# Values, states and the places of the down projections in a gated linear attention kernel with a SoLU block

## The chip, the cores and the metric

The kernel runs on one core of a Trainium2 chip. A time is device microseconds of one execution, from its start to its end. The profile is of one other execution of the same program on the same kind of chip, taken by the hardware profiler. PE is the engine for matrix products, DVE, ACT and POOL work on vectors, SP issues transfers.

## The reference

A recurrent attention with a gate for every key channel, then a two-layer block whose hidden values pass through a SoLU (value times softmax) and a layer norm. B=4 batches, H=8 heads, S=768 tokens, D=48 channels; 3072 tokens of 384 values, 1024 hidden.

```python
for t in range(S):
    state = alpha[:, :, t, :, None] * state + np.einsum('bhd,bhe->bhde', k[:, :, t], v[:, :, t])
    y[:, :, t] = np.einsum('bhd,bhde->bhe', q[:, :, t], state)
x = y.transpose(0, 2, 1, 3).reshape(B * S, H * D)
h = x @ w_in
e = np.exp(h - np.max(h, axis=-1, keepdims=True))
solu = h * (e / (np.sum(e, axis=-1, keepdims=True) + 1e-09))
mu = np.mean(solu, axis=-1, keepdims=True)
var = np.mean((solu - mu) ** 2, axis=-1, keepdims=True)
out = (solu - mu) / np.sqrt(var + 1e-06) * g_ln @ w_out
```

## The kernel before

The sequence is cut into G=6 chunks of 128 tokens; a chunk holds four batches, so 512 tokens. Within a chunk the attention is done by products: scaled queries times scaled keys, masked (`scores`, `masked`, giving sT), times v (`read_values`), plus scaled queries times the state of the chunks before (`read_state`). Both add into four PSUM banks y, one for each batch; ACT copies them to x. `next_state` multiplies the keys (turned back by `keys_back`) with v into two PSUM banks kv and adds them to the state; `decay` on POOL multiplies the state with the chunk's gate.

A head's 48 key channels don't fit 32 rows. They are kept as 32 firsts and 16 lasts; two heads' lasts share 32 rows, so there are H=8 blocks of firsts and NP=4 of lasts, NB=12 in all. On the side of the values, vn and the state have 80 columns for a head: 32 firsts, 16 zeros, 16 lasts, 16 zeros. `last` takes 32 columns that hold a head's lasts at the one end or the other, zeros at the rest, so that two heads add into the same 32 rows of y. The state has 16 blocks: 8 for the firsts of the keys, 8 for the lasts, where a pair of heads has both heads' keys in its rows; `apart` makes queries qv with zeros in the other head's rows from qe, which holds both. `read_state(n)`, n = 0 to 3, does one group of y's rows: n = 0, 1 the firsts of the values, n = 2, 3 the lasts of even and odd heads. A matrix product in fp32 stands in the profile as two matmuls and two weight loads.

The block after it: `up(g, f)`, f = 0 to 7, makes 128 hidden channels of chunk g for its 512 tokens (3 products of 512 columns), ACT takes the exponential, DVE multiplies it with h to u, ACT squares u. `running` sums over f on POOL and DVE, `token_sums` adds up over channels on PE. `down(n, half)` makes one batch's 128 tokens n of the output from four of the eight u blocks (4 products of 385 columns); `finish(n)` scales and stores it, for chunk 0 to 4 by SP.

Order is written out by hand; each engine runs its instructions in the order in which the program issues them. A prologue does chunk 0's attention, its ups and downs, and chunk 1's attention up to `next_state(1)`. Then the loop over g = 1 to 5, here called periods, does eight steps each: up(g, s), with work of the attention of chunk g+1 placed by a plan (`first` for period 1, `second` for 2, `usual` for 3 and 4; period 5 has none), and one half down of chunk g-1 per step, from the list `todo`. Within a step the places are head, up, finish, token sums, behind, running sums, middle, down, tail. Periods 2 to 5 thus hold eight half downs, period 1 none, and chunk 5's eight come after the loop, with the last chunk's token sums and norm behind the first.

In the old plans the values and the new state stand at step 7's tail, after the down; the new state is made for the last chunk too. The keys, with loading of v (`load_v`, by SP), come at step 0 behind the up.

Names and lines: down 471 to 480 (matmul 477), up_mm 366, up_act 380 to 382, running 394 and 397, scores 268, masked 279, keys_back 287 and 289, the matmuls of read_state and read_values both 300 (in `y_mm`), x copies 331, next_state 342 and 351, decay 251 and 254, queries 244, key transposes on DVE 184 and 187, scans 209, load_v 170.

Of the kernel before, what the change touches and what calls it, by code (L numbers as in the profile page):

```python
# [32 lines left out]
def fast_path(ctx, tc, q, k, v, alpha, moe_w_in, moe_w_out, moe_g_ln, out):  # L33
# [133 lines left out]
    def load_v(g):  # L167
        t = slice(g * P, (g + 1) * P)
        for dst, src in ((slice(0, E0), slice(0, E0)), (slice(48, 64), slice(E0, D))):
            nc.sync.dma_start(  # L170
                out=vn[:, :, :, dst].rearrange("p b h d -> p (b h) d"),
                in_=v[:, :, t, src].rearrange("b h p d -> p (b h) d"),
            )

    def load_v_first(slot):
        x = slots[slot].rearrange("p (n d) -> p n d", d=D)
        y = vn.rearrange("p b h d -> p (b h) d")
        nc.sync.dma_start(out=x, in_=v[:, :, 0:P].rearrange("b h p d -> p (b h) d"))
        for dst, src in ((slice(0, E0), slice(0, E0)), (slice(48, 64), slice(E0, D))):
            nc.gpsimd.tensor_copy(out=y[:, :, dst], in_=x[:, :, src])  # L180

# [111 lines left out]

    parts = [(a, [(NP * a + r, slice(0, E0)) for r in range(NP)]) for a in range(2)]
    parts += [(2, [(2 * r + i, last[i]) for r in range(NP)]) for i in range(2)]
# [37 lines left out]
    def next_state(g):  # L333
        kv = banks("kv", [H, 64], 2)
        for j in range(NB):
            for b in range(B):
                if j < H:
                    o, e = kv[0][quarter(b), j], vn[:, b, j, 0:64]
                else:
                    i = 2 * (j - H)  # L340
                    o, e = kv[1][quarter(b), i : i + 2], vn[:, b, i : i + 2, 0:64]
                nc.tensor.matmul(  # L342
                    o, lhsT=kg[:, j, quarter(b)], rhs=e, start=True, stop=True, tile_position=(0, 32 * b),
                    skip_group_check=True,
                )
# [283 lines left out]
    load_first(q, qn, 0)  # L629
    nc.gpsimd.memset(vn, 0.0)  # L630
    nc.gpsimd.memset(unit, 0.0)
# [151 lines left out]
    finish(3)  # L783
# [9 lines left out]
    first = dict(  # L793
        head={4: "keys_back", 6: "masked0", 7: "masked1"},
        behind={0: "v keys", 1: "on2 on0", 2: "on1 lasts", 3: "firsts", 4: "apart", 5: "decay", 7: "alpha"},
        tail={5: "scores0", 6: "scores1", 7: "begin read0 read1 read2 read3 values"},
        middle={},
    )
    second = dict(
        head={4: "keys_back", 6: "masked0", 7: "masked1"},  # L800
        behind={0: "back_late", 1: "v keys", 2: "on2 on0 on1", 3: "lasts firsts", 4: "apart", 5: "decay", 6: "alpha", 7: "back"},
        tail={5: "scores0", 6: "scores1", 7: "read2 read3 values"},
        middle={7: "begin read0 read1"},
    )

    def attend(a, what):
# [50 lines left out]
    todo = []  # L857
    for g in range(1, G + 1):
# [10 lines left out]
        for s in range(FC):  # L869
# [31 lines left out]
    for n, half in todo[2:4]:  # L901
        down(n, half)

# [24 lines left out]
    finish(G * B - 3)  # L928
    down(*todo[4])
    all_ok = ps_a.tile([P, 512], FP, tag="a0", name="all_ok")  # L930
# [4 lines left out]
    )  # L935
    down(*todo[5])
    finish(G * B - 2)
    down(*todo[6])
# [3 lines left out]
    down(*todo[7])  # L942
    finish(G * B - 1)
# [442 lines left out]
```

## Time and profile before

| | us |
|---|---|
| median of 14 runs | 407.2 |
| lowest, highest run | 402.6, 411.63 |
| the profiled execution | 401.82 |
| its span, first to last instruction | 400.0 |

| stretch of the span, us | what runs | PE busy | DVE busy | ACT busy | POOL busy |
|---|---|---|---|---|---|
| 113 to 157 | period 1 | 37.86 | 33.43 | 17.82 | 28.65 |
| 157 to 216 | period 2 | 58.61 | 43.49 | 19.17 | 21.44 |
| 216 to 273 | period 3 | 57.00 | 37.59 | 19.96 | 20.95 |
| 273 to 331 | period 4 | 58.00 | 31.33 | 16.73 | 21.09 |
| 331 to 400 | period 5 and the end | 64.17 | 23.91 | 14.62 | 13.97 |

The stretches are the periods, cut to whole microseconds at the start of their first up. A busy time near the stretch's length says that an engine hardly waits; it doesn't say that its instructions couldn't stand closer. Matmuls overlap, so what one costs is read from the starts of it and the next in the timeline, not from its duration. The granted clock of PE was 0.995 of full speed over the span.

### The profile page before, as it was taken

The page shows a single profiled execution, that of the slowest core. Times are in us where ns is not written, and L with a number is a line of the kernel's source. Part 1 is how long each engine was busy: PE and PEld are TensorE (multiplying, and loading weights), DVE is VectorE, ACT ScalarE, POOL GpSimd, SP SyncE. Part 2 cuts the span into 40 slices and gives each one's busy share as a digit, 9 for nine tenths or more (in the row PEclk, how much of TensorE's full clock was granted, in tenths as well). Part 3 has the DMA queues.
Part 4 walks back from the last instruction along what each step waited for, and adds up shares of the span by engine and source line. Part 5 has one row for each costly group of instructions (what it writes and reads, how often), then busy time and mean ns, then how long its engine had stood idle before and what let it go on. Part 6 is the DMA issues. An engine that isn't in the chain of part 4 may idle for free. (4 is left out here: it accounts for less than half of the span.)

```text
span 400.0 us, 11119 instructions
## 1 busy us (share of the span) xinstructions
PE 376.3 (94%) x4929; PEld 229.9 (57%) x4929; DVE 256.0 (64%) x415; ACT 146.3 (37%) x253; POOL 118.4 (30%) x118
## 2 busy tenths in 40 slices
PE   8698999769997798999999999999999999999995
PEld 8685355346753466554657555666556575555552
DVE  0989879996659882897782884664865413444510
ACT  2627773553532543223433243343152132223100
POOL 5020000030014993066510456210475110333200
PEclk9989999999999999999999999999999999999999
DMA  9966988304346305443030931004300000000011
GB/s 185 194 182 179 223 258 143 81 20 100 103 74 105 80 3 116 46 100 79 22 101 24 158 76 45 2 23 72 30 20 21 23 3 21 20 20 15 27 41 48
DMA packets 86409, 30.82 MB, mean 77 GB/s; under 512 B 67912, under 2 KB 84560, under 8 KB 86352
## 3 DMA queue, kind: packets, MB, share of 16 engines
q1 hardware_dynamic: 85328, 29.11, 34.0%
q8 instruction: 40, 0.66, 0.7%
q10 hardware_dynamic: 1024, 0.92, 0.7%
q14 instruction: 17, 0.14, 0.1%
HBM read 25.30 MB, written 4.72 MB: 75 GB/s over the span
## 5 line engine op out<-in xcount | busy, mean ns | idle before, releaser
L366 PE MATMUL h<-x,w_in 128*128 128x512 f32 x288 | 132.4, 600 | 4.7 <-DVE room L381 3.5
L477 PE MATMUL o<-w_out,room 128*128 128x385 f32 x384 | 133.2, 491 | 1.1 <-DVE least L223 1.1
L477 PEld LDWEIGHTS o<-w_out,room 128*128 128x128 f32 x384 | 71.4, 189 | 57.1 <-issue 15.2
L366 PEld LDWEIGHTS h<-x,w_in 128*128 128x128 f32 x288 | 52.6, 189 | 64.1 <-issue 49.4
L381 DVE TENSOR_TENSOR room<-h,e 128x512 f32<-128x512 f32 x40 | 27.6, 690 | 56.7 <-ACT e L380 56.6
L508 POOL TENSOR_TENSOR r<-sums,mhalf 128x1 f32<-128x1 f32 x20 | 12.2, 608 | 166.7 <-DVE sums L500 166.6
L380 ACT ACTIVATE e<-h 128x512 f32<-128x512 f32 x40 | 23.9, 597 | 82.1 <-PE h L366 82.1
L397 POOL TENSOR_TENSOR p<-p,e 128x512 f32<-128x512 f32 x30 | 42.2, 1405 | 21.8 <-ACT e L380 21.7
L382 ACT ACTIVATE u<-room 128x512 f32<-128x512 f32 x40 | 25.2, 630 | 50.3 <-DVE room L381 50.3
L279 DVE TENSOR_TENSOR sT<-a,mask 128x512 f32<-128x512 f32 x44 | 27.3, 684 | 11.8 <-PE a L268 11.8
L268 PE MATMUL a<-qv,kT 32*128 32x128 f32 x704 | 25.9, 288 | 5.5 <-DVE least L223 2.1
L268 PEld LDWEIGHTS a<-qv,kT 32*128 32x128 f32 x704 | 22.9, 194 | 12.6 <-issue 3.4
L397 DVE TENSOR_TENSOR p<-p,u 128x512 f32<-128x512 f32 x30 | 24.1, 803 | 7.0 <-ACT u L382 7.0
L209 DVE TENSOR_TENSOR_SCAN hT<-aT,unit 128x516 f32<-128x516 f32 x18 | 21.8, 1256 | 8.9 <-ACT aT L655 8.8
L209 DVE TENSOR_TENSOR_SCAN aT<-aT,seed 128x516 f32<-128x516 f32 x18 | 24.9, 1386 | 0.6
L351 DVE TENSOR_TENSOR state<-state,kv 128x512 f32<-128x512 f32 x10 | 6.9, 688 | 27.4 <-PE kv L342 27.4
L300 PE MATMUL y<-sT,vn 128*32 128x128 f32 x768 | 22.9, 274 | 1.0 <-issue 0.5
L331 ACT COPY x<-y 128x384 f32<-128x384 f32 x24 | 11.5, 480 | 32.1 <-PE y L300 32.1
L233 POOL TENSOR_TENSOR kT<-kT,hT 128x1024 f32<-128x1024 f32 (+1 forms) x8 | 13.7, 1741 | 31.3 <-DVE kT L184 31.3
L300 PEld LDWEIGHTS y<-sT,vn 128*32 128x32 f32 x768 | 20.8, 110 | 3.4 <-issue 2.5
L300 PE MATMUL y<-qv,state 32*32 32x128 f32 x1280 | 20.1, 278 | 1.7 <-issue 1.3
L300 PEld LDWEIGHTS y<-qv,state 32*32 32x32 f32 x1280 | 15.9, 103 | 9.2 <-issue 6.2
(140 smaller groups left out, 394.1 us busy)
## 6 DMA issues: line engine op xcount, KB each, us to landing
an<-in_alpha_dram SPq DMA_DIRECT2D x20, 192.0 KB, 4.1
out_dram<-o_sb SPq DMA_DIRECT2D x20, 192.0 KB, 1.9
room<-in_moe_w_out_dram SPq DMA_DIRECT2D x8, 384.0 KB, 4.1
kn<-in_k_dram SPq DMA_DIRECT2D x16, 192.0 KB, 4.3
qn<-in_q_dram SPq DMA_DIRECT2D x16, 192.0 KB, 3.6
vn<-in_v_dram SPq DMA_DIRECT2D x5, 512.0 KB, 5.8
room<-in_moe_w_in_dram SPq DMA_DIRECT2D x16, 128.0 KB, 4.0
kn<-in_k_dram SPq DMA_DIRECT2D x4, 384.0 KB, 5.8
```

The source lines that it names most:

```text
L209: nc.vector.tensor_tensor_scan(out=o, data0=a, data1=s, initial=1.0, op0=ALU.mult, op1=ALU.add)
L233: nc.gpsimd.tensor_tensor(out=kT[:, part], in0=kT[:, part], in1=hk[:, part], op=ALU.mult)
L268: nc.tensor.matmul(a[b][:, i], lhsT=kT[quarter(b), kb], rhs=qv[quarter(b), qb], start=kb == h, stop=kb != h, tile_position=(32 * b, 0), sk ...
L279: nc.vector.tensor_tensor(out=sT[:, b, half * NP : half * NP + NP], in0=a[b], in1=mask[:, None, :].to_broadcast([P, NP, P]), op=ALU.mult,)
L300: nc.tensor.matmul(y_bank(b)[quarter(r), a], lhsT=lhsT, rhs=rhs, start=(b, r) not in begun, stop=stop, tile_position=(row, 32 * r), skip_g ...
L366: nc.tensor.matmul(h, lhsT=w_in[:, a, f * P : (f + 1) * P], rhs=d["x"][:, a].rearrange("p b t -> p (b t)"), start=(a == 0), stop=(a == KC ...
L380: nc.scalar.activation(out=e, in_=h, func=AF.Exp)
L381: nc.vector.tensor_tensor(out=u, in0=h, in1=e, op=ALU.mult)
L382: nc.scalar.activation(out=u2, in_=u, func=AF.Square)
L397: eng.tensor_tensor(out=p, in0=d[0][i] if f == 1 else p, in1=d[f][i], op=ALU.add)
L477: nc.tensor.matmul(d["o"][:, 0 : DM + 1], lhsT=u_of(g, f)[:, b * P : b * P + P], rhs=w_out[:, f], start=(f == 0), stop=(f == FC - 1), skip ...
L508: nc.gpsimd.tensor_tensor(out=r, in0=s[:, 3:4], in1=mhalf, op=ALU.pow)
```

## The change

Five edits.

1. vn and the state have 64 columns a head. An even head has its 48 values in columns 0 to 47, an odd one in 16 to 63 with the lasts ahead of the firsts, so that `last` is columns 32 to 63 or 0 to 31, again with zeros at the other end. The products of `next_state` take 48 columns instead of 64, for pairs 96 instead of 128 (from a tile vt that is vn with 32 columns behind it). Loading v takes four transfers or copies instead of two; the state's adds and decays go by even and odd heads, four instead of two or three.
2. `decay` also makes ends_state on POOL: for each pair of heads the lasts by lasts part of the state, with the other head's rows made zero. `read_state(2)` multiplies it with qe for both heads at once, and `read_state(3)` does no product with the lasts of the keys.
3. The half downs stand one place sooner: the first of chunk g in step 7 of period g, the last of them in step 6 of period g+1. After the loop the token sums stand behind the second half down of chunk 5.
4. The values stand in the middle of step 7, between its up and its down; the new state of chunk a-1 ("states") in step 0 of the next period, behind the up and ahead of loading v. In periods 1 and 2 all reads stand right before the values. In the prologue down(3, 1) moves behind the values.
5. The last chunk makes no new state and turns no keys back.

```diff
-    VW = 80
-    vn = const.tile([P, B, H, VW], FP, name="vn")
+    VW = 64
+    vt = const.tile([P, B * H * VW + 32], FP, name="vn")
+    vn = vt[:, 0 : B * H * VW].rearrange("p (b h d) -> p b h d", b=B, h=H)
     state = const.tile([P, 2 * H, VW], FP, name="state")
-    last = [slice(48, 80), slice(32, 64)]
+    ends_state = const.tile([P, NP, 2, E1], FP, name="ends_state")
+    all_of = [slice(0, D), slice(E1, VW)]
+    first_of = [slice(0, E0), slice(E0, 2 * E0)]
+    last_of = [slice(E0, E0 + E1), slice(E1, E0)]
+    last = [slice(E0, 2 * E0), slice(0, E0)]
...
-        for dst, src in ((slice(0, E0), slice(0, E0)), (slice(48, 64), slice(E0, D))):
-            nc.sync.dma_start(
-                out=vn[:, :, :, dst].rearrange("p b h d -> p (b h) d"),
-                in_=v[:, :, t, src].rearrange("b h p d -> p (b h) d"),
-            )
+        for dst, src in ((first_of, slice(0, E0)), (last_of, slice(E0, D))):
+            for i in range(2):
+                nc.sync.dma_start(
+                    out=vn.rearrange("p b (h i) d -> p i (b h) d", i=2)[:, i, :, dst[i]],
+                    in_=v[:, i::2, t, src].rearrange("b h p d -> p (b h) d"),
+                )
...
-        s = state[:, 0:H, 0:64]
-        nc.gpsimd.tensor_tensor(out=s, in0=s, in1=h4[:, 0:H, 1:2].to_broadcast([P, H, 64]), op=ALU.mult)
         for i in range(2):
-            s = state[:, H : 2 * H, 0:64].rearrange("p (j i) e -> p j i e", i=2)[:, :, i]
-            nc.gpsimd.tensor_tensor(out=s, in0=s, in1=h4[:, H:NB, 1:2].to_broadcast([P, NP, 64]), op=ALU.mult)
+            for rows, d in ((0, h4[:, i:H:2, 1:2]), (H, h4[:, H:NB, 1:2])):
+                s = state[:, rows + i : rows + H : 2, all_of[i]]
+                nc.gpsimd.tensor_tensor(out=s, in0=s, in1=d.to_broadcast([P, NP, D]), op=ALU.mult)
+            nc.gpsimd.tensor_scalar(
+                out=ends_state[:, :, i], in0=state[:, H + i : 2 * H : 2, last_of[i]], scalar1=parity[:, i : i + 1],
+                scalar2=None, op0=ALU.mult,
+            )
...
         for rows in (0, H):
+            if rows and n == 3:
+                break
             for r, (h, e) in enumerate(hs):
                 for b in range(B):
                     p = quarter(b)
-                    y_mm(b, a, r, 32 * b, state[p, rows + h, e], qv[p, rows + h])
+                    if rows and n == 2:
+                        s, q = ends_state[p, r].rearrange("p i d -> p (i d)"), qe[p, r]
+                    else:
+                        s, q = state[p, rows + h, e], qv[p, rows + h]
+                    y_mm(b, a, r, 32 * b, s, q)
...
-        for i in range(2):
-            s = state[:, H * i : H * i + H, 0:64]
-            if g == 0:
-                nc.scalar.copy(out=s, in_=kv[i])
-            else:
-                nc.vector.tensor_tensor(out=s, in0=s, in1=kv[i], op=ALU.add)
+        for n in range(2):
+            for i in range(2):
+                s, x = state[:, H * n + i : H * n + H : 2, all_of[i]], kv[n][:, i::2]
+                if g == 0:
+                    nc.scalar.copy(out=s, in_=x)
+                else:
+                    nc.vector.tensor_tensor(out=s, in0=s, in1=x, op=ALU.add)
...
-    read_state(0)
-    read_state(1)
-    down(3, 1)
-    read_state(2)
-    read_state(3)
+    for n in range(4):
+        read_state(n)
     alpha_over(2)
...
     read_values(1)
-    next_state(1)
+    down(3, 1)
     finish(3)
...
     usual = dict(
...
-        behind={0: "v keys", 1: "on2 on0 on1", 2: "lasts firsts", 3: "apart", 5: "decay", 6: "alpha", 7: "back"},
-        tail={4: "scores0", 5: "scores1", 6: "begin read0 read1", 7: "values"},
-        middle={7: "read2 read3"},
+        behind={0: "states v keys", 1: "on2 on0 on1", 2: "lasts firsts", 3: "apart", 5: "decay", 6: "alpha", 7: "back"},
+        tail={4: "scores0", 5: "scores1", 6: "begin read0 read1"},
+        middle={7: "read2 read3 values"},
...
-        tail={5: "scores0", 6: "scores1", 7: "begin read0 read1 read2 read3 values"},
-        middle={},
+        tail={5: "scores0", 6: "scores1"},
+        middle={7: "begin read0 read1 read2 read3 values"},
...
-        behind={0: "back_late", 1: "v keys", 2: "on2 on0 on1", 3: "lasts firsts", 4: "apart", 5: "decay", 6: "alpha", 7: "back"},
-        tail={5: "scores0", 6: "scores1", 7: "read2 read3 values"},
-        middle={7: "begin read0 read1"},
+        behind={0: "states back_late", 1: "v keys", 2: "on2 on0 on1", 3: "lasts firsts", 4: "apart", 5: "decay", 6: "alpha", 7: "back"},
+        tail={5: "scores0", 6: "scores1"},
+        middle={7: "begin read0 read1 read2 read3 values"},
...
-        elif what == "keys_back":
+        elif what == "keys_back" and more:
             keys_back(a)
...
             read_values(a)
-            next_state(a)
+        elif what == "states":
+            next_state(a - 1)
...
-    todo = []
+    todo = [None] * (FC - 1)
...
-            if todo:
-                n, half = todo.pop(0)
+            if rise and s == FC - 1:
+                todo.append((g * B, 0))
+            step = todo.pop(0)
+            if step:
+                n, half = step
                 down(n, half)
...
-        todo = [(n, half) for n in range(g * B, g * B + B) for half in range(2)]
+        todo = [(n, half) for n in range(g * B, g * B + B) for half in range(2)][1:]
...
-    for n, half in todo[:2]:
-        down(n, half)
-        if half == 0:
-            token_sums(G - 1)
-            last_norm()
+    last = iter(todo)
+    down(*next(last))
+    token_sums(G - 1)
+    last_norm()
+    down(*next(last))
     finish(G * B - B)
```

More of the change, by code (lines that the diff above doesn't have):

```diff
@@ L177, in load_v_first @@
         y = vn.rearrange("p b h d -> p (b h) d")
+        xi, yi = (z.rearrange("p (n i) d -> p i n d", i=2) for z in (x, y))
         nc.sync.dma_start(out=x, in_=v[:, :, 0:P].rearrange("b h p d -> p (b h) d"))
-        for dst, src in ((slice(0, E0), slice(0, E0)), (slice(48, 64), slice(E0, D))):
-            nc.gpsimd.tensor_copy(out=y[:, :, dst], in_=x[:, :, src])
+        for dst, src in ((first_of, slice(0, E0)), (last_of, slice(E0, D))):
+            for i in range(2):
+                nc.gpsimd.tensor_copy(out=yi[:, i, :, dst[i]], in_=xi[:, i, :, src])
     def firsts(src, dst):
@@ L289, in keys_back @@
             nc.scalar.copy(out=kg[:, NP * i : NP * i + NP], in_=t[i])
-    parts = [(a, [(NP * a + r, slice(0, E0)) for r in range(NP)]) for a in range(2)]
+    parts = [(a, [(NP * a + r, first_of[r % 2]) for r in range(NP)]) for a in range(2)]
     parts += [(2, [(2 * r + i, last[i]) for r in range(NP)]) for i in range(2)]
@@ L333, in next_state @@
     def next_state(g):
-        kv = banks("kv", [H, 64], 2)
+        kv = banks("kv", [H, D], 2)
         for j in range(NB):
@@ L337, in next_state @@
                 if j < H:
-                    o, e = kv[0][quarter(b), j], vn[:, b, j, 0:64]
+                    o, e = kv[0][quarter(b), j], vn[:, b, j, all_of[j % 2]]
                 else:
                     i = 2 * (j - H)
-                    o, e = kv[1][quarter(b), i : i + 2], vn[:, b, i : i + 2, 0:64]
+                    at = (b * H + i) * VW
+                    e = vt[:, at : at + 160].rearrange("p (i d) -> p i d", i=2)[:, :, 0:D]
+                    o = kv[1][quarter(b), i : i + 2]
                 nc.tensor.matmul(
@@ L345, in next_state @@
                 )
-        for i in range(2):
-            s = state[:, H * i : H * i + H, 0:64]
-            if g == 0:
-                nc.scalar.copy(out=s, in_=kv[i])
-            else:
-                nc.vector.tensor_tensor(out=s, in0=s, in1=kv[i], op=ALU.add)
+        for n in range(2):
+            for i in range(2):
+                s, x = state[:, H * n + i : H * n + H : 2, all_of[i]], kv[n][:, i::2]
[3 more added lines that the diff above has]
+                    nc.vector.tensor_tensor(out=s, in0=s, in1=x, op=ALU.add)
     def u_of(g, f):
@@ L629, in fast_path @@
     load_first(q, qn, 0)
-    nc.gpsimd.memset(vn, 0.0)
+    nc.gpsimd.memset(vt, 0.0)
     nc.gpsimd.memset(unit, 0.0)
@@ L794, in fast_path @@
         head={4: "keys_back", 6: "masked0", 7: "masked1"},
-        behind={0: "v keys", 1: "on2 on0", 2: "on1 lasts", 3: "firsts", 4: "apart", 5: "decay", 7: "alpha"},
-        tail={5: "scores0", 6: "scores1", 7: "begin read0 read1 read2 read3 values"},
-        middle={},
+        behind={0: "states v keys", 1: "on2 on0", 2: "on1 lasts", 3: "firsts", 4: "apart", 5: "decay", 7: "alpha"},
+        tail={5: "scores0", 6: "scores1"},
+        middle={7: "begin read0 read1 read2 read3 values"},
     )
@@ L891, in fast_path @@
             finish(after)
-        todo = [(n, half) for n in range(g * B, g * B + B) for half in range(2)]
-    for n, half in todo[:2]:
-        down(n, half)
-        if half == 0:
-            token_sums(G - 1)
-            last_norm()
+        todo = [(n, half) for n in range(g * B, g * B + B) for half in range(2)][1:]
[4 more added lines that the diff above has]
+    down(*next(last))
     finish(G * B - B)
-    for n, half in todo[2:4]:
-        down(n, half)
+    down(*next(last))
     parts = [N * 3, G * 2, G * NB] + [len(pieces)] * 2
@@ L928, in fast_path @@
     finish(G * B - 3)
-    down(*todo[4])
+    down(*next(last))
     all_ok = ps_a.tile([P, 512], FP, tag="a0", name="all_ok")
@@ L935, in fast_path @@
     )
-    down(*todo[5])
+    down(*next(last))
     finish(G * B - 2)
-    down(*todo[6])
+    down(*next(last))
     taken = nc.values_load(
@@ L941, in fast_path @@
     )
-    down(*todo[7])
+    down(*next(last))
     finish(G * B - 1)
```

## The prediction

> **What bounds the kernel now.** I read the busy shares first, then PE's own timeline from end to end, then DVE's timeline wherever PE waits, and last the DMA queues.
>
> ```profile
> PE 376.3 (94%) x4929; PEld 229.9 (57%) x4929; DVE 256.0 (64%) x415; ACT 146.3 (37%) x253; POOL 118.4 (30%) x118
> ```
>
> A busy share of 94% doesn't prove a bound; the timeline does. From 157 us to 376 us PE starts nearly every group as the one before ends. This is the end of period 3 and the start of period 4 (columns: start, us, engine, line, operation, count):
>
> ```profile
> 255.87 2.76 PE L477 MATMUL o<-w_out,room 128*128 128x385 f32 x8
> 258.56 1.90 PE L300 MATMUL y<-qv,state 32*32 32x128 f32 x128
> 260.39 2.84 PE L366 MATMUL h<-x,w_in 128*128 128x512 f32 x6
> 263.16 1.90 PE L300 MATMUL y<-qv,state 32*32 32x128 f32 x128
> 264.99 2.86 PE L477 MATMUL o<-w_out,room 128*128 128x385 f32 x8
> 267.78 3.70 PE L300 MATMUL y<-sT,vn 128*32 128x128 f32 x128
> 271.30 1.95 PE L342 MATMUL kv<-vn,kg 128*32 128x64 f32 x96
> 273.18 2.84 PE L366 MATMUL h<-x,w_in 128*128 128x512 f32 x6
> ```
>
> Start to start, half the state reads take 1.83 us, the values 3.52, the new state (kv) 1.88. An instruction removed here shortens the kernel by its spacing. Period 1 is different (a bracket is the idle time before the row, and what ended it):
>
> ```profile
> 127.52 2.84 PE L366 MATMUL h<-x,w_in 128*128 128x512 f32 x6 [2.66 <-DVE room L381]
> 131.19 2.84 PE L366 MATMUL h<-x,w_in 128*128 128x512 f32 x6 [0.82 <-DVE room L381]
> 134.79 0.50 PE L268 MATMUL a<-qv,kT 32*128 32x128 f32 x8 [0.76 <-POOL qv L244]
> ```
>
> ```profile
> 117.11 2.03 DVE L184 STREAM_TRANSPOSE kT<-kn 128x1024 f32<-128x1024 f32 x1
> ```
>
> From this transpose on DVE has no idle time up to 135 us, and PE waits for it, or for POOL and ACT behind it: 2.66+0.82+0.76, and 0.51 for ACT, 4.75 us. What counts there is when DVE starts. Before 90 us DVE bounds too (PE waits 2.02 us for it at 89.78). There is a third kind of stall:
>
> ```profile
> 107.42 2.93 PE L300 MATMUL y<-sT,vn 128*32 128x128 f32 x99 [0.54 <-issue]
> ...
> 111.43 1.63 PE L342 MATMUL kv<-vn,kg 128*32 128x64 f32 x70 [0.63 <-issue]
> ...
> 151.10 0.41 PE L300 MATMUL y<-qv,state 32*32 32x128 f32 x4 [1.29 <-issue]
> ```
>
> ```profile
> q8 instruction: 40, 0.66, 0.7%
> ```
>
> No engine releases these. Between the first two starts stand 128 matmuls by the timeline's counts (99+2+3+24), each with a weight load: 256 instructions. Between the second and the third stand 510 matmuls, near four times 128. The queue moved 40 packets of 16 KB. So I read them as instruction blocks that arrive late in long runs of small matmuls.
>
> **The change, part by part** (against the profiled execution's 401.82 us).
>
> *Dropped for the last chunk.* Its kv: 1.88 us (328.77 to 330.65). Its key transposes: 12 matmuls, 294.74 to 296.04, 1.30 us. Both lie in the dense stretch: **3.18 us**. Three ACT copies and two DVE adds go too, off the path.
>
> *Block-diagonal reads.* The last two groups take 96 matmul records instead of 128: 32 x 14.3 ns (1.83 us/128) = 0.46 us a chunk, five chunks.
>
> *Narrower kv.* The 32 double-head records go from 128 to 96 columns. Four of them start every 0.109 us; a quarter less in 8 fours is 0.22 us a chunk. The 64 single ones go from 64 to 48 columns; a window of 0.90 us holds 62 of them, 58 ns per four. By columns, a quarter of 16 fours would go: 0.23 us. The Trainium skill ("TensorE: Matmul & The Clock Gate", Back-to-back issue gap) says that 1 to 64 columns cost the same: 0. The nearest row sides with it: the reads, with 128 columns, also come 14.3 ns apart, so columns don't set this spacing. I take 0; the other end is 0.9 us more over four chunks (8.9 instead of 8.0 in the sum). Chunk 0's kv (at 35.28) lies before the wait for DVE at 89.78: nothing.
>
> *Mode edges.* A down between two ups takes 2.59 us start to start, between two tiled groups 2.79 (264.99 to 267.78); an up 2.57 against 2.77. So each edge between full and tiled matmuls costs 0.10, while reads running into values (208.47 to 210.31, 1.84) cost nothing. From step 6's down to step 0's down a usual period has eight edges and gets six, the second plan six and gets four: 0.2 us at the end of periods 2, 3 and 4. The others keep theirs.
>
> *Entering period 1.* Reads start at 99.34 as now and take 1.83+1.37, to 102.55; values to 106.1; down(3,1) to 108.95; then up(1,0), which starts at 112.99 now. x is ready: ACT ends its alpha work at 104.1 and the fourth copy near 106.9. Exp and DVE's product follow as now (3.51 us after the start, 0.69 long), to 113.2. Then come the four state adds, which stand on DVE ahead of the key transposes and wait for kv, queued on PE behind up(1,0): up ends at 111.7, kv at 113.4. Adds of 192 columns, estimated from DVE rows of 128 (0.35) and 512 (0.69), come about 0.35 us apart and end at 114.6. The transposes start then, not at 117.11: **2.5 us**, which holds this chunk's reads, its narrow kv and both old issue stalls (1.17). PE does kv in time in which it waited for DVE.
>
> *After it.* Period 1's reads 0.46; periods 2 and 3 each 0.46+0.22+0.2 = 0.88; period 4 0.88+3.18 = 4.06. With the 2.5 that is 8.78.
>
> *Issue stalls.* The old 1.29 goes with its order: 10.07. But reads and values now run unbroken in chunks 1 to 3, 224+128 = 352 matmuls; in two of these a down stood between. The skill's "Runtime: NRT & Kernel Launch" (Instruction fetch mechanics) says that blocks of 256 instructions are fetched ahead and that the crossing is mostly hidden; by it no stall comes and the gain is 10.07. The rows say that a block used up faster than about 4.0 us (107.42 to 111.43) isn't covered in a long run: reads use one in 1.83 us, values in 3.52. I take 0.8 entering period 1, 0.8 at its end, 0.5 at period 2's end (each between 0 and 1.29), none later, where an up still divides the reads: -2.1. **Sum: 8.0 us.**
>
> *What hides the rest.* The last x copy on ACT ends 0.73 us after the values (272.03 against 271.30); kv's 1.88 hid it, a down's 2.86 does: 0, uncovered 0.73 a period. At step 0 kv and the adds come behind up and token sums; in period 2 they hold DVE's scans 0.3 us, and DVE later idles 3.99 us: 0. decay on POOL, 1.06+1.20 us, becomes four of 0.49 and two of 0.26 (estimates from these rows): +0.2; it ends 11 us before the reads in period 3, 2.9 in period 1: 0. SP issues four v transfers instead of two, with the same packets; they landed in 5.2 to 7.7 us, start about 3 us later in the period, and are needed some 40 us on. Behind them on SP stand key loads and output stores that nobody awaits soon: 0. The first v copies on POOL (20.45 to 22.75) have 2.5 us to the first values, and the smaller memsets lie before an idle stretch: 0. After the token sums six half downs follow instead of seven, the seventh having gone into step 7; the check's total is ready 4.3 us after them and asked for after three halves, 8.0: 0. The first down of period 1 needs w_out's centred blocks 0 to 3, ready on POOL at 146.6: 0.
>
> **Rivals.**
> 1. *Blocks arrive in time*: gain 10.1, 397.1 us. For it: no such stall at 208 to 216, where 352 matmuls ran. Against: three stalls now. Chance 0.2.
> 2. *Period 1's earlier start isn't carried*: POOL, ACT or a late load of keys keeps the queries where they are; the 2.5 goes, 5.5 stays: 401.7. For it: PE's later waits there name POOL and ACT. Against: both stand behind DVE's transposes. Chance 0.15.
> 3. *Slower, instruction blocks bound every run of reads and values*: two stalls of 1.29 in each of five is 12.9 us against 10.07: +2.8, 410.0. It decides once such stalls pass 10.1 us. Against: usual periods keep an up between, and have none now. Chance 0.06.
> 4. *It doesn't do what it says*: x copies or PSUM banks hold each period's first up longer than kv did; gain near 0, 407. Chance 0.05.
>
> The forecast itself has 0.54.
>
> **How the numbers follow.** The profiled execution (401.82, of which 400.0 are the span) lies below all 14 runs shown (median 407.2); I carry the difference: 407.2 - 8.0 = **399.2 us**. The low end takes a gain of 11.0 (rival 1 and the kv columns) and 1 us of drift in a median: 395.2. The high end takes rival 2 and 2 us of drift: 403.6. Half a percent, 2 us, is what a measurement can tell from none. Faster by more: the forecast, rival 1 and most of rival 2, 0.87; within: rival 4 and a bit, 0.06; slower: rival 3 and a bit, 0.07.
>
> **What would show it.** Right: 4661 matmuls (4929-160-96-12); the second half of the reads in 1.37 us; period 1's key transposes about 2.5 us earlier; from period 2 on no wait of an up for x. Wrong: ups at step 0 that wait for ACT's copies; state adds after which those transposes start later than 116.5; issue stalls of over 10 us in sum.

## The result, and the profile after

The changed kernel takes 398.38 us in the median of 10 runs (396.77 to 404.22), the kernel before 407.28 in 47 runs (402.13 to 411.63): a ratio of 0.983, with a 95% interval of 0.979 to 0.988, so 5 to 8.5 us. The ratio leaves out the slowest executions of each kernel, those more than 1.5% above its fastest; the plain quotient of the two medians is 0.978. The forecast was 399.2. The profiled executions lie closer together: 397.71 us (span 395.76) against 401.82 (400.02), 4.26 us of span. So the median falls about as far as predicted, but the profiled pair only about half as far: stalls took more than the working allowed, and some gains that it didn't count give a part of that back.

In the changed kernel's profile the matmuls of reads and values stand at line 314, the new state (kv) at 364, up at 389, token sums at 455 and down at 500. From its page, busy time, share and instructions of each engine, then the queue that loads instructions:

```profile
PE 371.4 (94%) x4661; PEld 224.6 (57%) x4661; DVE 253.2 (64%) x421; ACT 144.3 (36%) x252; POOL 127.2 (32%) x135
...
q8 instruction: 38, 0.62, 0.7%
```

PE has exactly the 4661 matmuls counted beforehand and the same 94%. What has grown stands in the view of waits (waiting instruction, releaser: us in total, times, longest):

```profile
PE y L314 <- issue: 6.1, 5, 2.8
```

The three issue stalls that the prediction counted, 2.46 us, have become five of 6.1 us. The first two stand at the entry of period 1 (PE's timeline, start and duration in us):

```profile
101.76 0.40 PE L314 MATMUL y<-qe,ends_state 32*32 32x128 f32 x15 [1.15 <-issue]
...
105.49 1.95 PE L314 MATMUL y<-sT,vn 128*32 128x128 f32 x62 [0.59 <-issue]
107.37 2.86 PE L500 MATMUL o<-w_out,room 128*128 128x385 f32 x8
```

Between the two starts lie 128 matmuls with their 128 weight loads. With all records of PE's queue counted from the start of the trace, its few semaphore waits too, each of the five stalls begins at number 450 + 256k (2754, 3010, 4034, 4290, 5570), and so do the three of before (3010, 3266, 4290). The packets of the queue that loads instructions (q8, 16 KB each) say what PE waits for. All times in us, from the trace of the changed kernel:

| stall at number | PE passes the boundary before | q8 packet starts | it lands | PE goes on |
|---|---|---|---|---|
| 2754 | 98.71 | 99.42 | 100.40 | 101.76 |
| 3010 | 101.76 | 102.89 | 103.90 | 105.49 |
| 4034 | 144.45 | 145.20 | 146.10 | 147.64 |
| 4290 | 147.64 | 148.68 | 149.56 | 151.09 |
| 5570 | 203.23 | 205.54 | 206.71 | 208.04 |

In all 14 profiles 66 of the 70 issue stalls lie at such a number, and each of the 66 ends 1.20 to 1.61 us after its packet lands. The other four are taken up at e10.

The largest stall ends period 2:

```profile
208.04 0.30 PE L314 MATMUL y<-qe,ends_state 32*32 32x128 f32 x2 [2.80 <-issue]
...
208.93 5.17 PE L314 MATMUL y<-sT,vn 128*32 128x128 f32 x128
214.02 2.86 PE L500 MATMUL o<-w_out,room 128*128 128x385 f32 x8
```

The values behind it take 5.09 us from start to start instead of 3.52. The view by windows says why (stretch and its length, busy time of PE, PEld, DVE, ACT and POOL, granted clock, DMA share, GB/s):

```profile
202.00:206.00 4.00, 3.24 (x190) 2.33 (x189) 3.18 (x7) 1.27 (x3) 1.50 (x2) 1.00 0.84 191
206.00:210.00 4.00, 1.96 (x57) 1.47 (x60) 3.41 (x3) 0.54 (x1) 1.74 (x1) 0.82 0.15 53
210.00:214.00 4.00, 4.00 (x114) 3.68 (x104) 0.00 (x0) 1.44 (x3) 0.00 (x0) 0.75 0.02 4
```

By the trace's clock record it drops to half for 3.4 us, from 208.57 to 211.98, right after PE stood idle: a stall of 2.80 us costs 4.37. Ahead of it the DMA engines are 0.84 busy, with the alpha load of chunk 5, and the q8 packet starts 2.31 us after the boundary before, where the other four took 0.71 to 1.13.

The end of period 3 is what a period looks like without such a stall:

```profile
266.07 0.50 PE L314 MATMUL y<-qv,state 32*32 32x128 f32 x32
...
267.48 3.70 PE L314 MATMUL y<-sT,vn 128*32 128x128 f32 x128
271.11 2.86 PE L500 MATMUL o<-w_out,room 128*128 128x385 f32 x8
273.81 2.74 PE L389 MATMUL h<-x,w_in 128*128 128x512 f32 x6
...
276.95 1.52 PE L364 MATMUL kv<-vn,kg 128*32 128x48 f32 x96
278.40 2.86 PE L500 MATMUL o<-w_out,room 128*128 128x385 f32 x8
```

The second half of the reads takes 1.41 us, the new state 1.45 instead of 1.88, and the up behind the down starts with no wait for x.

Where the 4.26 us come from. The predicted column books the prediction's own terms by stretch: the new state of each chunk moves out of one period's end into the next one's start, and one half down (2.70 us) from the end of the kernel into period 1.

| stretch | before, us | after, us | predicted difference | measured |
|---|---|---|---|---|
| start to the first chunk's main scores (89.78) | 89.78 | 88.71 | 0 | -1.07 |
| from there to period 1's main scores (135.80) | 46.02 | 45.07 | -1.70 | -0.95 |
| from there to period 2's first up | 21.14 | 22.10 | -0.13 | +0.96 |
| period 2 | 58.77 | 60.84 | -0.38 | +2.08 |
| period 3 | 57.48 | 57.09 | -0.88 | -0.39 |
| period 4 | 57.47 | 55.12 | -2.18 | -2.35 |
| period 5 and the end | 69.37 | 66.83 | -2.70 | -2.54 |
| sum | 400.02 | 395.76 | -7.97 | -4.26 |

### The profile page after: what moved, and what is told of

It reads as the page before. It is cut to its first block, busy times and chain, and to the rows that moved or that the text cites. A ratio compares the mean times of both kernels' runs of the same rounds, so it can differ in the third digit from the quotient of the medians.

```text
span 395.8 us, 10612 instructions
## 1 busy us (share of the span) xinstructions
PE 371.4 (94%) x4661; PEld 224.6 (57%) x4661; DVE 253.2 (64%) x421; ACT 144.3 (36%) x252; POOL 127.2 (32%) x135
## 5 line engine op out<-in xcount | busy, mean ns | idle before, releaser
L531 POOL TENSOR_TENSOR r<-sums,mhalf 128x1 f32<-128x1 f32 x20 | 14.7, 736 | 162.7 <-DVE sums L523 162.7
L220 DVE TENSOR_TENSOR_SCAN hT<-aT,unit 128x516 f32<-128x516 f32 x18 | 23.0, 1327 | 9.0 <-ACT aT L678 8.9
L314 PE MATMUL y<-sT,vn 128*32 128x128 f32 x768 | 24.7, 285 | 1.5 <-issue 1.1
L420 DVE TENSOR_TENSOR p<-p,u 128x512 f32<-128x512 f32 x30 | 22.4, 745 | 5.6 <-ACT u L405 5.6
L314 PEld LDWEIGHTS y<-sT,vn 128*32 128x32 f32 x768 | 22.0, 115 | 3.8 <-issue 2.7
L220 DVE TENSOR_TENSOR_SCAN aT<-aT,seed 128x516 f32<-128x516 f32 x18 | 23.7, 1318 | 0.6
L212 ACT ACTIVATE sq<-an,mone 128x1536 uint8<-128x1536 f32 x12 | 18.8, 1570 | 0.2
L314 PE MATMUL y<-qv,state 32*32 32x128 f32 x960 | 16.3, 278 | 1.1 <-issue 1.1
L314 PEld LDWEIGHTS y<-qv,state 32*32 32x32 f32 x960 | 12.0, 103 | 6.7 <-issue 4.2
```

What stands on the lines that cost most here:

```text
L212: nc.scalar.activation(out=sq, in_=x, func=AF.Relu, scale=sign, bias=mone, accum_out=over[:, g, i : i + 1])
L220: nc.vector.tensor_tensor_scan(out=o, data0=a, data1=s, initial=1.0, op0=ALU.mult, op1=ALU.add)
L314: nc.tensor.matmul(y_bank(b)[quarter(r), a], lhsT=lhsT, rhs=rhs, start=(b, r) not in begun, stop=stop, tile_position=(row, 32 * r), skip_g ...
L420: eng.tensor_tensor(out=p, in0=d[0][i] if f == 1 else p, in1=d[f][i], op=ALU.add)
L531: nc.gpsimd.tensor_tensor(out=r, in0=s[:, 3:4], in1=mhalf, op=ALU.pow)
```

## The experiments

All were profiled on the same kind of chip, most timed against runs of the kernel before beside them. A time without an interval is a median.

### The parts alone

**e1, the drop alone.** The kernel before with only edit 5.

```diff
-        elif what == "keys_back":
+        elif what == "keys_back" and more:
...
-            next_state(a)
+            if more:
+                next_state(a)
```

> The kernel before, without the new state and the turned keys of the last chunk (neither is read). Theory (PE's dense stretch sets the end there): 1.88+1.30 = 3.2 us less, ratio 0.992, and the same three issue stalls as before (2.5 us in all). Rival (the work dropped was covered by something else): no change, ratio 1.000.

Measured: 404.66 us against 405.1, ratio 0.998 (0.994 to 1.003): not told from none. In the profile period 4 is 2.41 us shorter (55.06 against 57.47), and 1.71 come back behind the last instruction of ACT, where the last store lands 5.6 us after its issue instead of 3.9, which the edit doesn't touch. Why not 3.18 in period 4 shows PE's timeline:

```profile
325.12 3.70 PE L300 MATMUL y<-sT,vn 128*32 128x128 f32 x128
329.42 2.84 PE L366 MATMUL h<-x,w_in 128*128 128x512 f32 x6 [0.60 <-ACT x L331]
```

The up starts 4.30 us after the values, not 3.52. Taking kv away uncovers the last x copy, for 0.77 us. The prediction put the uncovered cost at 0.73 and trusted a down to hide it; in the changed kernel, with that down, no wait of an up for x is left. The part alone loses a quarter of its 3.18 us. Another 1.2 us more than in the first profile of before lie ahead of period 4, where the edit changes nothing, so the span as a whole (400.50) isn't shorter.

**e2, the layout alone.** Edits 1 and 2, with the old order and nothing dropped.

```diff
-    VW = 80
+    VW = 64
...
-        kv = banks("kv", [H, 64], 2)
+        kv = banks("kv", [H, D], 2)
...
+            if rows and n == 3:
+                break
```

> The kernel before with 64-column values and states and the block-diagonal state alone; order, downs and the last chunk's work as before. Theory by the traces of before and after: reads 0.42 us less in five chunks, kv 0.41 less in five of which chunk 0's is lost to DVE: 3.7 to 4.2 us less, ratio 0.990; issue stalls about as before, 2 to 3 us. Rival by the prediction's rule (1 to 64 columns cost the same): kv goes from 1.88 to 1.66 only, 3.2 us less in all. Rival of the wasted start (DVE sets period 1): 1 us of these doesn't arrive.

Measured: 405.9 us, ratio 1.001 (0.998 to 1.005): nothing, where 3.7 to 4.2 us were expected. Periods 3 and 4 are each 0.85 us shorter, just what the reads (1.83 to 1.41) and kv (1.88 to 1.45) give. But kv stands right behind the values here, and at the entry of period 1 and the ends of periods 1 and 2 it runs dry:

```profile
112.64 0.95 PE L364 MATMUL kv<-vn,kg 128*32 128x48 f32 x38 [1.23 <-issue]
...
159.44 0.94 PE L364 MATMUL kv<-vn,kg 128*32 128x48 f32 x36 [2.05 <-issue]
...
219.40 0.36 PE L364 MATMUL kv<-vn,kg 128*32 128x96 f32 x4 [0.91 <-issue]
```

All issue stalls come to 7.05 us against 2.46, which eats the gain. In a run of small matmuls that waits for its instructions, shorter matmuls only make the wait longer.

**e3, the order alone.** Edits 3 to 5 with the old 80 columns.

```diff
-        middle={7: "read2 read3"},
+        middle={7: "read2 read3 values"},
...
+        elif what == "states":
+            next_state(a - 1)
```

> The changed order alone, with 80-column values and states and no block-diagonal state; it also drops the last chunk's work. Theory (instruction blocks come late in unbroken runs): runs of 256+128 matmuls entering period 1 and at the ends of periods 1 and 2 stall 5 to 8 us in all, against 2.5 before; 3.2 for the drop, 0.6 for mode edges and about 2 for the earlier start of period 1's DVE chain remain against 3 to 5 more stall: 1 to 4 us less, ratio 0.990 to 0.998. Rival (the stalls don't depend on the order): 5.8 us less and more, ratio 0.986.

Measured: 403.54 us, ratio 0.996 (0.993 to 0.999). The stalls come to 6.1 us, five of them, the longest 1.56. So the drop gains 0.2% (not told from none), the layout nothing, the order with the drop 0.4%, and all together 1.7%. The new layout is worth nothing in the old order and about 1.3% in the new one, which takes kv out of the run behind the values. That this move is what sets it free was not tried alone.

### The stalls

**e4 and e7, the changed kernel twice more.** No edit: is the stall of 2.80 us at the end of period 2 there in every execution?

> The changed kernel again, beside the next three on one chip: 397 to 400 us; issue stalls in its profile between 3 and 6 us, at the same three places if they belong to the order of instructions.

> The changed kernel once more, as the measure for the next three on the same chip: ratio to before 0.980 to 0.988; the stall in period 2's reads 2.3 to 2.8 us, those of period 1 1.1 to 1.3 and about 0.5.

Measured: 400.57 us, ratio 0.983 (0.975 to 0.992), and 399.37, ratio 0.986 (0.979 to 0.992). The stall is there each time, 2.34 and 2.57 us long, at the same instruction number. Behind 2.57 the clock is halved as in the first profile (period 2 is 60.52 us); behind 2.34 it isn't (59.34). The record holds the reason. Within each execution the stretches of half clock begin a whole number of steps of 3.413 us apart (44 stretches in 14 profiles), and the clock is halved when enough idle time of PE falls within one step. First profile, then e4, by these steps:

```profile
205.16:208.57 3.41, 0.61 (x40) 0.47 (x35) 3.41 (x3) 0.58 (x1) 2.58 (x2) 1.00 0.20 68
208.57:211.98 3.41, 3.41 (x64) 2.83 (x65) 0.84 (x2) 0.48 (x1) 0.00 (x0) 0.50 0.02 5
```

```profile
209.63:213.04 3.41, 1.75 (x133) 1.46 (x121) 3.34 (x7) 1.21 (x2) 2.40 (x2) 1.00 0.47 100
213.04:216.46 3.42, 2.73 (x110) 2.47 (x112) 2.52 (x2) 0.48 (x1) 0.85 (x1) 1.00 0.17 62
```

The stall of 2.80 us lies whole in one step; that of 2.34 is cut by the end of its step, and only 1.66 us of idle time fall within it. Where the steps lie differs from execution to execution. So stalls can be relied on, half clock can't.

**e5, a longer run.** Periods 3 and 4 get the plan's long run as well: all reads right before the values.

```diff
-        tail={4: "scores0", 5: "scores1", 6: "begin read0 read1"},
-        middle={7: "read2 read3 values"},
+        tail={4: "scores0", 5: "scores1"},
+        middle={7: "begin read0 read1 read2 read3 values"},
```

> The changed kernel with the reads of periods 3 and 4 unbroken too: the first half moves from step 6 to step 7, right before the second half and the values (352 matmuls in a run at five places instead of three). Theory (a run that uses an instruction block of 256 faster than it is fetched stalls): issue stalls of 1 to 2.8 us appear in periods 3 and 4, where there are none now; less 0.4 for fewer mode edges, it is 1.5 to 4 us slower than the changed kernel. Rival (the stalls come from traffic or chance at their places): none in periods 3 and 4, 0.4 us faster.

Measured: 400.93 us against 400.57 for e4 beside it, which so few runs don't tell apart. The profile does: a stall appears in period 3, where the changed kernel has none, and the values behind it are slow (5.30 us from start to start).

```profile
269.49 0.37 PE L314 MATMUL y<-qv,state 32*32 32x128 f32 x2 [1.86 <-issue]
269.79 5.37 PE L314 MATMUL y<-sT,vn 128*32 128x128 f32 x128
275.09 2.86 PE L500 MATMUL o<-w_out,room 128*128 128x385 f32 x8
```

Period 3 takes 60.60 us instead of 57.09. Period 4, with the same order, takes 55.39 instead of 55.12, with a stall of 0.22. So the same run costs 3.5 us or 0.3. Where the multiples of 256 fall in it differs between the two periods; whether that alone decides was not tried.

**e6, the runs of periods 1 and 2 cut.** A half down between read 1 and read 2 there, and the new state right after the values again ("now").

```diff
-        tail={5: "scores0", 6: "scores1"},
-        middle={7: "begin read0 read1 read2 read3 values"},
+        tail={5: "scores0", 6: "scores1", 7: "read2 read3 values now"},
+        middle={7: "begin read0 read1"},
```

> The changed kernel with a half down between the two halves of the reads at the ends of periods 1 and 2, and there the new state right behind the values as before (it covers the x copies); entering period 1 as in the changed kernel. Theory: the stalls at the ends of periods 1 and 2 (1.08+0.46 and 2.80 in the changed kernel's profile, and the half clock after the last) shrink to under 1 us each; 0.2 us of mode edges is added at each; 1 to 4 us faster than the changed kernel where those stalls come, ratio to before 0.975 to 0.983. Rival: stalls stay where they are, 0.4 us slower than the changed kernel.

Measured: 398.2 us, ratio 0.983 (0.974 to 0.992), no better than e4 within what these runs tell. The large stall of period 2 goes: the period takes 58.62 us instead of 59.34 to 60.84. But period 1 takes 48.20 instead of 45.97 in e4. Of these 2.2 us 1.45 are the new state itself, which stands in period 1 here and at the start of period 2 there; the rest is a longer stall, which has moved to kv:

```profile
158.92 1.03 PE L364 MATMUL kv<-vn,kg 128*32 128x48 f32 x45 [2.48 <-issue]
```

The q8 packet of this stall starts 2.73 us after the boundary before. The clock stays full: the stall is cut by the end of a step, like that of e4. A cut helps only when what is behind it isn't made longer.

**e8, the alpha load later.** In the changed kernel, the loading of chunk 5's alpha, in flight before the 2.80 us, is issued some steps later, in the next period's step 1.

```diff
-            if a + 2 < G:
-                load(alpha, an, a + 2)
+        elif what == "alpha_in" and more:
+            load(alpha, an, a + 1)
```

> The changed kernel with the gates of chunks 4 and 5 loaded in step 1 of periods 2 and 3, not right ahead of the reads of periods 1 and 2. Theory (period 2's instruction block came 1 us later than others because its fetch stood behind this load, DMA share 0.84 there): the stall in period 2's reads falls from 2.3-2.8 to 1.0-1.5 us, period 1's changes little; about 1 us faster than the changed kernel, 3 where the half clock follows the long stall. Rival (only the order of instructions decides): 2.3 to 2.8 stays and the time is the same.

Measured: 399.85 us, ratio 0.985 (0.978 to 0.992), the same as e7 beside it. In the profile period 2's stall falls apart:

```profile
212.17 0.30 PE L314 MATMUL y<-qe,ends_state 32*32 32x128 f32 x2 [1.75 <-issue]
...
216.18 1.28 PE L314 MATMUL y<-sT,vn 128*32 128x128 f32 x36 [0.45 <-issue]
```

2.20 us instead of 2.57, no half clock, and the period 1.5 us shorter than in e7; against e4, which had no half clock there either, it is 0.3 shorter. The q8 packet starts 1.42 us after the boundary before, against 1.87 in e4 and e7 and 2.31 in the first profile. So the load lengthens the stall at this boundary by 0.6 to 1.1 us, of which a part comes back at the next, and isn't its only cause: 1.75 are left with the DMA engines almost idle (a share of 0.00 to 0.03 from 204 to 212 us).

**e9 and e10, all runs cut, without and with the later load.** From the changed kernel: a half down between read 1 and read 2 in periods 1 and 2 and in the prologue, kv staying in step 0, and in periods 2 and 3 the token sums ahead of the first up.

```diff
-    for n in range(4):
-        read_state(n)
+    read_state(0)
+    read_state(1)
+    down(3, 1)
+    read_state(2)
+    read_state(3)
...
-        tail={5: "scores0", 6: "scores1"},
-        middle={7: "begin read0 read1 read2 read3 values"},
+        tail={5: "scores0", 6: "scores1", 7: "read2 read3 values"},
+        middle={7: "begin read0 read1"},
...
+            if s == 0 and g in (2, 3):
+                token_sums(g - 1)
```

> The changed kernel with a half down between the two halves of the reads at all three unbroken places (entering period 1, ends of periods 1 and 2); the values then run straight into the next period's first up, with only token sums between at the ends of periods 1 and 2. Theory: stalls there fall from about 6 us to 1 to 3; the up now waits up to 0.8 us for the last x copy at each place and 0.2 goes for mode edges: 1 to 3 us faster than the changed kernel. Rival: the x waits and edges (up to 3 us) take what the stalls give: no change.

> Both of the last two edits: if stalls add up as told, 1 to 4 us faster than the changed kernel, and the fastest of the four.

Measured: e9 397.09 us, ratio 0.979 (0.972 to 0.985); e10 394.72, ratio 0.974 (0.968 to 0.980), the fastest of all; its interval overlaps that of the changed kernel beside it (e7, 399.37, 0.979 to 0.992) by a thousandth. e10's end of period 2:

```profile
201.82 1.91 PE L314 MATMUL y<-qv,state 32*32 32x128 f32 x128
203.66 2.86 PE L500 MATMUL o<-w_out,room 128*128 128x385 f32 x8
...
207.87 3.92 PE L314 MATMUL y<-sT,vn 128*32 128x128 f32 x128
212.40 0.65 PE L455 MATMUL rows<-p,ones 128*32 128x64 f32 x32 [0.61 <-issue]
```

The down stands between the halves of the reads. The boundary that cost 2.80 us (5570) is crossed at 207.07 and the next (5826) at 210.28, with no stall that the view lists. The 0.61 at the token sums is of another kind, like 0.64 at the end of period 1 and two in e9: it lies at none of the numbers 450 + 256k, and the weight load there starts 0.07 us after ACT's last x copy ends (212.30 to 212.37). It is the wait for x that e9's expectation named, and what a cut at this place costs. Period 2 takes 57.48 us instead of 60.84, and from the first main scores to the end the kernel takes 302.08 instead of 307.05. The changed kernel's other two profiles have 307.76 and 307.05 here. Same work, another order: the stalls and what follows them were worth about 5 us.

### The kernel before, twice more

**e11 and e12.** No edit to the kernel before. The question: why do the medians lie further apart than the first profiles?

> The kernel before, profiled once more, for a question left by the medians: its profiled execution (401.82 us, granted clock 0.995) lies 5 us below its median, while the changed kernel's (397.71, clock 0.983) lies within 1 us of its own. Over 56 executions of the kernel before, 0.01 less granted clock goes with 3.2 us more. Theory: stretches of 3.4 us at half clock fall where PE is the bound, at the first up (31 to 40 us) and near the scores and reads at 93 us, as in profiles of its variants; an execution at 0.988 or less then takes 405 to 409 us, with the first up's wait at 3 to 4 us instead of 1.2 and up to 1.6 us more between 89 and 99 us, and its five periods and end (310.2 us from the main scores group to the end) within 1 us of the first profile. Rival: the extra time lies in the periods themselves, at the issue stalls (2.46 us in the first profile), which would then be over 5 us.

> The same once more, since an execution's granted clock can't be chosen: at 0.993 or more, 402 to 404 us and the first profile's stage lengths within 0.5 us each; at 0.988 or less, the longer stages named for the run beside it.

Measured: 404.59 us at a granted clock of 0.987, and 402.31 at 0.994. e12 agrees with the first profile in every stage to 0.3 us, and its stall in period 1 is 1.55 us. e11 is 2.8 us longer, and 2.47 of it lie in period 1 (46.42 against 43.95 us):

```profile
152.32 0.41 PE L300 MATMUL y<-qv,state 32*32 32x128 f32 x4 [2.11 <-issue]
152.66 5.37 PE L300 MATMUL y<-sT,vn 128*32 128x128 f32 x128
157.84 1.95 PE L342 MATMUL kv<-vn,kg 128*32 128x64 f32 x96
```

The theory of a slow start falls for this execution: up to 99 us e11 and the first profile agree within 0.2 us. The rival's place is right, though the stalls come to 3.5 us and not over 5: it is one longer stall, 2.11 instead of 1.29, and the half clock behind it. So the kernel before pays for the same thing in part of its executions. Over the 73 of its timed executions whose clock is on record, the 38 with 0.99 or more of the clock have a median of 403.7, the other 35 one of 407.7; the changed kernel's 19 below 0.99 have 399.4, its 3 at or above it 397.1.

## Why the prediction was right, point by point

**Dropped for the last chunk (3.18): right, with its condition.** Period 4 gives 2.35: 1.30 are the key transposes, 0.42 the narrower reads, and 0.43 is what kv(4), which moves in at the period's start, is shorter than kv(5), which is gone from its end. The 0.2 left is what the prediction gave the mode edges. e1 shows that without the down the term would have been 2.41.

**Block-diagonal reads (0.46 a chunk): right.** 1.41 us measured for the second half, 1.37 predicted.

**Narrower kv (0.22 a chunk): too small.** It is 0.43. The double records shrink by a quarter as reckoned (0.109 us for four to 0.083). The single ones do too: four start every 43 ns, against 56 in the trace of before (the prediction's 58 came from a window). The step that failed is the one that weighed a count by columns against the Trainium skill's rule of equal cost for 1 to 64 columns ("TensorE: Matmul & The Clock Gate", Back-to-back issue gap), and took the reads, with 128 columns at 14.3 ns, as the nearest row. They use tiles of 32 rows and 32 columns where kv's have 128 rows; that this is why they don't compare was not tested. For kv the measurement goes by columns. The other end, 0.9 us over four chunks, was the right one.

**Entering period 1 (2.5 with the old stalls, less 0.8 for new): mechanism right, stall larger.** Relative to the first main scores DVE's key transposes start 0.91 us sooner; the new stalls there are 1.74 and not 0.8, and with them taken out it is 2.65. DVE's timeline shows the order that was foreseen:

```profile
113.47 0.69 DVE L404 TENSOR_TENSOR room<-h,e 128x512 f32<-128x512 f32 x1 [2.13 <-ACT e L403]
114.08 1.14 DVE L374 TENSOR_TENSOR state<-state,kv 128x192 f32<-128x192 f32 x4
115.13 2.01 DVE L195 STREAM_TRANSPOSE kT<-kn 128x1024 f32<-128x1024 f32 x1
```

Predicted were 113.2, adds until 114.6 and the transposes there. The scores behind them start 2.02 us sooner (133.78 against 135.80), as the transposes do (1.98): rival 2, that the earlier start isn't carried, is out. The gain of this stretch isn't the same in every execution: from the first main scores to those of period 1 e7 takes 45.27 us and e4 47.31, with half clock from 93.6 us on, where the three profiles of before have 46.02 to 46.30.

**Start of the kernel (0): 1.07 missed.** The wait for DVE at 89.78 was taken as hiding chunk 0's narrower kv; the main scores now come at 88.71, and only 0.4 of it is kv's own. The rest wasn't looked into. And the start varies more than that. In the first profile, as in all three of before (89.71 to 89.82), PE waits 1.22 us for the first up; in e4 and e7, with the kernel unchanged, it waits 4.16 and 3.26, half clock follows, and the main scores come at 92.48 and 92.31.

**Issue stalls (-2.1 for three): the term that was mis-sized most.** Five, 6.1 us, and 1.57 of half clock behind one: -7.7. The places were right (entering period 1, end of periods 1 and 2, none in 3 and 4), and that late blocks of 256 are the cause is shown by the instruction numbers, by the q8 packets that land just ahead of each stall's end, and by e5 to e10. The size was taken from two short stalls of before. The bound set for one stall, 1.29, fell, and the half clock wasn't thought of. Rival 1, that the blocks arrive in time, is refuted, and with it, for such runs, the mostly hidden crossing of the Trainium skill ("Runtime: NRT & Kernel Launch", Instruction fetch mechanics). Rival 3 had the mechanism, but not in every run of reads and values: 6.1 us, 7.7 with the half clock, stay below the 10.1 from which it decides.

**What hides the rest: right, with two small terms missed.** x, decay, v and the end of the kernel show no wait. In period 2 the waits for masked scores, 1.29 us of PE in all (202.57 to 205.69 instead of 1.83), are gone, since the reads now come 1.03 us later after the period's start and DVE is ready. In period 3 one scores group takes 2.66 us instead of 2.00, of which a wait for ACT's copy of the keys is 0.20.

So in the profiled pair the predicted 8.0 stand against 4.26. Stalls and half clock beyond the 2.1 take 5.6; kv's other half (0.8 over four chunks), the start (1.07) and the masked scores (1.29) give 3.2; the scores group takes 0.66: 8.0 - 5.6 + 3.2 - 0.7 = 4.9, and the 0.6 to 4.26 is not accounted for. (The high end of the forecast, rival 2 and 2 us of drift, adds up to 403.7, not 403.6.) That the medians lie 8.9 apart all the same, and the ratio says 6.8, has a part that is shown: the step from the profiled execution to the median, taken over unchanged, is itself partly stall and half clock (e11), and differs between the kernels. How the executions of before at 407 us and more spend their last 2 us was not seen in any profile and stays open. A slow start is one candidate: e1, with the same start, waits 3.43 us for the first up. From the first main scores to the end, where all of the 8.0 was to come from, the three profiles of before take 310.24, 312.98 and 310.81 us and those of the changed kernel 307.05, 307.76 and 307.05, so 2.5 to 5.9 us less. The forecast within 1 us is thus partly luck: its mechanism was right, its largest cost was put at about a quarter of the true one (2.1 against 7.7).

## What to carry to other kernels

Where PE runs hundreds of tiny matmuls in a row, count instructions before counting time: here, where a run waited, the next 256 of them (weight loads count) could be used 3 to 5 us after the last, and a longer run that uses them up faster waits, however short its matmuls are. Put a large product between two such runs, as e10 does; inside a run that waits, narrower matmuls gain nothing, as e2 shows. Look for what the removed work was hiding (x behind kv), and take several profiles before trusting a difference of 1%: where the steps of the clock fall is different in each execution.

## What the runs showed of the hardware

- PE stalls at boundaries of 256 instructions once a long run uses blocks faster than they come. At a stall the boundary is crossed 3.05 to 4.81 us after the one before (98.71 to 101.76, 101.76 to 105.49, 147.64 to 151.09 and 203.23 to 208.04 in the changed kernel), while reads alone would use a block in 1.83 us and values in 3.52. After a slow block one fast block passes free: 321.26 to 323.74, 2.48 us, without a stall. The longest distance fell where DMA was 0.84 busy. In the five the 16 KB packet starts 0.71 to 2.31 us after the boundary before and takes 0.9 to 1.2, and PE goes on 1.33 to 1.59 us after it has landed.
- A stall of about 2 us can be enough for 3.4 us at half clock: seen after 1.86, 2.11, 2.57 and 2.80 us, not after 1.75, 2.05, 2.34 or 2.48. What fits all of these is how much of the stall falls within one step of 3.413 us. From 95 us on the 14 profiles hold 1214 such steps: all 12 with 1.99 us or more of PE idle are followed by half clock, of the two between 1.8 and 1.9 the one with 1.86 is and the one with 1.88 isn't, and none with less is. Ahead of 95 us, with other matmuls, the same holds from 2.0 us up, but some steps with about 1.5 us idle are followed by half clock too. This agrees with the free-running window of 3.4 us that the Trainium skill describes ("TensorE: Matmul & The Clock Gate", Part 1: The HAM clock gate).
- Where PE waits for DVE anyway, the half clock costs nothing that could be seen: in period 1 of the changed kernel the clock is halved from 126.65 to 130.06, after a wait of 2.00 us for DVE, and the scores still come as early as DVE's start asks.
- Four fp32 matmuls in four column tiles of PE, with 128 rows, start every 56 ns at 64 columns and every 43 at 48 (kv before and after).
